# First chunks of x and w1 cut into three transfers, two of them on ScalarE's queue, and the products of two chunks ordered by terms

## The chip, the cores and the metric

The kernel runs on one core of a Trainium2 chip. The metric is device time in microseconds (us): the median of several executions. One execution was also profiled, and every row shown here is of that one.

## The reference

The block mixes two branches of the same x (2048 rows, D = 448) by a gate per row:

```
g = sigmoid(sum(x * gate_w))
a = linear_attention(x; wqkv, wo)        # 16 heads, phi(t) = where(t > 0, t + 1, exp(t)) + 1e-6
h = x @ w1 + b1;  r = max(h, 0);  b = (r * r) @ w2 + b2        # w1: 448 x 1792
out = g * a + (1 - g) * b
```

All data are float32. What the change touches is the very first product, h = x @ w1 for the first 512 rows of x.

## The kernel before

Every float32 operand is split into a high part (a copy into the type that TensorE multiplies at full pace, called `hi`, `xh`, `w[:, c]`) and a low part (the float32 value minus the high part: `lo`, `xl`, `w[:, 4 + c]`). A product is then three matmuls: high x high, high x low and low x high. ScalarE (ACT) or VectorE (DVE) makes the high part, VectorE the low one.

x comes in transposed blocks of 512 rows (`TB`), each cut along the contracted dimension into 4 chunks of 128 partitions (c = 0 to 3). w1 comes in halves and groups of columns; group 0 of half 0 has 512 columns, 4 tiles of 128 (f = 0 to 3), and 4 chunks as well. The start of the program computes the four tiles `h_ps` (f = 0 to 3, `first`) of block 0. It begins with 14 matmuls on constants (`warm_ps`, L177), which need no data. Then chunk 0: its halves of x and w1 lie beside each other in one tensor `xw` of two parts, loaded by SyncE's queue (SP) into `xw_raw[0]` and `xw_raw[1]`. Part 0 holds 256 of the 512 columns of x and 256 of the 512 columns of w1, part 1 the rest. From part 0 ScalarE makes `xh[:, :256]` and VectorE `w[:, 0, :256]`; then the tiles f = 0 and 1 are multiplied with 256 columns each (L547), again for part 1, and then all that is left of chunk 0 with 512 columns (L229 in `up_chunk`): the high products of f = 2 and 3, the four `xl` products and the four of w1's low part. Chunks 1 to 3 follow, f by f with all terms of an f together. After them come the key product (`k_ps`) and the second product of the same block (`o_ps`).

TensorE, ScalarE and VectorE execute in the order in which the program is written. The order on SP is settled by the scheduler of the framework, which is free to put a transfer that waits for nothing ahead of others. A transfer occupies the queue while it is issued. SP and ScalarE can each issue transfers. Raw inputs share 15 buffers (`slot`); `gw_s` (gate_w, copied to all 128 partitions) and `b1_s` have buffers of their own.

Of the kernel before, what the change touches and what calls it, by code (L numbers as in the profile page):

```python
# [7 lines left out]
F = mybir.dt.float32  # L8
R = mybir.dt.float32r
AF = mybir.ActivationFunctionType  # L10
# [5 lines left out]
P = 128  # L16
TB = 512
# [8 lines left out]
def f32(ap):  # L26
    return ap.bitcast(F)


@with_exitstack  # L30
def gated_mix_kernel(ctx: ExitStack, tc: tile.TileContext, xw, xt, xn, wk, wq, wv, wo, w1a, w1b, w2, b1, b2, gw,
                     hmask, kvmask, halves, out):
    nc = tc.nc
    act, dve, pool, pe, sp = nc.scalar, nc.vector, nc.gpsimd, nc.tensor, nc.sync
# [6 lines left out]
    rest = ctx.enter_context(tc.tile_pool(name="rest", bufs=1, side="right"))  # L41
# [6 lines left out]
    def bank(name):  # L48
        turn[0] ^= 1
        return ms_p.tile([P, 512], F, name=name, tag=f"ms{turn[0]}")  # L50
# [3 lines left out]
    def slot(shape, dt, name):  # L54
        return work.tile(shape, dt, name=name, tag="s", bufs=NSLOT)

    def load(dst, src):
        sp.dma_start(out=dst, in_=src)
# [4 lines left out]
    def split_hi(eng, hi, src):  # L63
        if eng is act:
            act.activation(hi, src, AF.Copy)  # L65
        elif eng is pool:
            pool.tensor_scalar(hi, src, 1.0, 0.0, op0=ALU.mult, op1=ALU.add)
        else:
            eng.tensor_copy(hi, src)  # L69

    def split_lo(eng, lo, src, hi):
        eng.tensor_tensor(lo, src, f32(hi), op=ALU.subtract)  # L72
# [29 lines left out]
    x_raw, xs = {}, {}  # L102

    def load_x(b, c):
        x_raw[b, c] = slot([P, TB], F, f"xr{b}_{c}")
        load(x_raw[b, c], xt[b, c])

    def new_x(b):
        return [keep.tile([P, 4, TB], R, name=f"x{p}{b}", tag=f"x{p}", bufs=2) for p in "hl"]

    def split_x(b, c):
        if c == 0:
            xs[b] = new_x(b)
        (xh, xl), r = xs[b], x_raw[b, c]
        if c < 3:
            split_hi(act, xh[:, c], r)
            split_lo(dve, xl[:, c], r, xh[:, c])
        else:
            split_last(xh[:, 3], xl[:, 3], r, side)
# [8 lines left out]

    w1_s, w1_raw = {}, {}

    def load_w1(h, g, c):
        w1_raw[h, g, c] = slot([P, (TB, 3 * P)[g]], F, f"w1r{h}{g}{c}")
        load(w1_raw[h, g, c], (w1a, w1b)[g][h, c])

    def new_w1(h, g):
        n, a, z = ((TB, 0, 16), (3 * P, 48, 0))[g]
        w = keep.tile([P, a + 7 * n + z], R, name=f"w1_{h}{g}", tag=f"w1{g}", bufs=1)
        w1_s[h, g] = w[:, a:a + 7 * n].rearrange("p (c n) -> p c n", c=7)
        return w1_s[h, g]

    def split_w1(h, g, c):
        if c == 0:
            new_w1(h, g)
        split_w(w1_s[h, g], c, w1_raw.pop((h, g, c)), act, dve)
# [7 lines left out]
    def split_w2(f):  # L152
        w2_s[f] = keep.tile([P, 2, D], R, name=f"w2_{f}", tag="w2", bufs=NH)
        split_hi(act, w2_s[f][:, 0], w2_raw[f])
        split_lo(dve, w2_s[f][:, 1], w2_raw.pop(f), w2_s[f][:, 0])
# [20 lines left out]
    for _ in range(14):  # L176
        pe.matmul(warm_ps[:, :256], warm[:, :P], warm, start=True, stop=True)  # L177

    side = rest.tile([P, 56], F, name="side")[:, :2]
    dve.memset(side[:64, 0:1], -1.0)  # L180
    dve.memset(side[:64, 1:2], 0.0)
    dve.memset(side[64:], 1.0)

    xw_raw = []
    for n in range(2):
        xw_raw.append(slot([P, TB], F, f"xwr{n}"))
        load(xw_raw[n], xw[n])
    for c in range(1, 4):
        load_x(0, c)
        load_w1(0, 0, c)  # L190
    b1_s = keep.tile([P, NF], F, name="b1_s")
    half = keep.tile([P, 2], F, name="half")
    ones = keep.tile([P, 2], F, name="ones")
# [8 lines left out]
    for c in range(4):  # L202
        load_w1(0, 1, c)
# [14 lines left out]
    def up_chunk(ps, b, f, c, only=None):  # L218
        h, fl = divmod(f, NH)
        g, i = divmod(fl, 4)  # L220
        w, cols = w1_s[h, g], slice(i * P, (i + 1) * P)
        xh, xl = xs[b]
        if c < 3:
            terms = [(w[:, c, cols], xh[:, c]), (w[:, c, cols], xl[:, c]), (w[:, 4 + c, cols], xh[:, c])]
        else:
            terms = [(w[:, 3, cols], xh[:, 3]), (w[:, 3, cols], xl[:, 3])]
        for n, (a, m) in enumerate(terms):
            if only in (None, n):
                pe.matmul(ps, a, m, start=(c == 0 and n == 0), stop=(c == 3 and n == 1))  # L229
# [155 lines left out]
    kv, wv_s, kvm = [], [], []  # L385

    def load_kv(c):
        if c == 0:
            kvm.append(slot([JE, D], F, "kvm"))
            load(kvm[0], kvmask)  # L390
        wv_s.append(slot([P, D], F, f"wv{c}"))
        load(wv_s[-1], wv[c])

    def kv_product():
        kv_ps = bank("kv_ps")
        z_ps = mm_p.tile([P, 512], F, name="z_ps", tag="mm")
        for c in range(4):
            pe.matmul(z_ps[:, 2 * c:2 * c + 2], zks[0][:, c].rearrange("p j r -> p (j r)"), ones, start=True,  # L398
                      stop=True)
        dve.tensor_copy(zc, z_ps[:, 0:8:2])  # L400
        for j in range(NJ):
            js = slice(j * JE, (j + 1) * JE)
            for c in range(4):
                pe.matmul(kv_ps[:JE, js], wv_s[c][:, js], gsum[c][:, js], start=(c == 0), stop=(c == 3))  # L404
        raw = slot([JE, D], F, "kv_raw")
        dve.tensor_tensor(raw, kv_ps[:JE, :D], kvm[0], op=ALU.mult)
        return raw.rearrange("p (j k) -> p j k", j=NJ)
# [126 lines left out]

    first = [mm_p.tile([P, 512], F, name=f"h_ps0_{f}", tag="mm") if f < 2 else bank(f"h_ps0_{f}") for f in range(4)]
    for c in range(4):
        if c == 0:
            xs[0] = new_x(0)  # L540
            w, (xh, xl) = new_w1(0, 0), [x[:, 0] for x in xs[0]]
            sides = slice(0, TB // 2), slice(TB // 2, TB)
            for n, cols in enumerate(sides):
                split_hi(act, xh[:, cols], xw_raw[n][:, sides[0]])
                split_hi(dve, w[:, 0, cols], xw_raw[n][:, sides[1]])
                for f in range(2):
                    pe.matmul(first[f][:, cols], w[:, 0, f * P:(f + 1) * P], xh[:, cols], start=(n == 0), stop=False)  # L547
            for m, (lo, hi) in enumerate(((xl, xh), (w[:, 4], w[:, 0]))):
                for n, cols in enumerate(sides):
                    split_lo(dve, lo[:, cols], xw_raw[n][:, sides[m]], hi[:, cols])  # L550
        else:
            split_x(0, c)
            split_w1(0, 0, c)
        if c == 0:
            for n in range(3):
                for f in range(0 if n else 2, 4):
                    up_chunk(first[f], 0, f, c, n)
        else:
            for f in range(4):
                up_chunk(first[f], 0, f, c)  # L560
    split_w2(0)
    split_w2(1)
    wk_s = keep.tile([P, 7, D], R, name="wk_s", tag="wkm", bufs=1)
# [53 lines left out]
    for b in range(1, NB):  # L617
        for f in range(NH):
# [36 lines left out]
            if b == 2:  # L655
# [4 lines left out]
                if f == 5:  # L660
                    raw = slot([P, P], F, "hmr")
# [3 lines left out]
            if b == 3:  # L665
                if f < 4:
                    load_w1(1, 0, f)
                if f == 4:
                    for c in range(4):
                        split_w1(1, 0, c)  # L670
                if f >= 2:
                    load_w2(NH + f - 2)
                if f >= 3:
                    split_w2(NH + f - 3)
                if f == 5:
                    key_sums()
                if f >= 5:
                    load_kv(2 * f - 10)
                    load_kv(2 * f - 9)
# [5 lines left out]
    for n, b in enumerate(order):  # L685
        then = order[n + 1] if n + 1 < NB else None
        for f in range(NF - NH, NF):
# [43 lines left out]
            if n == 0:  # L731
                if fl < 4:
                    todo += queries(b, (3, 0, 1, 2)[fl])
                if fl == 0:
                    for c in range(4):
                        load_w1(1, 1, c)
                    raw = kv_product()
# [91 lines left out]
```

## Time and profile before

| | |
|---|---|
| median of 3 executions | 435.35 us (435.15 to 435.68) |
| profiled execution, its own time | 435.59 us |
| span in the profile, first to last instruction | 433.8 us |
| TensorE (PE) matmul busy | 429.5 us, 99% |
| VectorE busy | 283.7 us, 65% |
| ScalarE busy | 174.5 us, 40% |
| GpSimd busy | 72.1 us, 17% |
| mean of the transfers | 67 GB/s |

The profiled execution took 1.8 us more than its span, and its time lies 0.24 us above the median. Matmuls are pipelined, so their recorded durations overlap: what one costs is the distance from its start to the next start, and a busy share of 99% says that there is hardly a gap, not that the clock is high.

### The profile page before, as it was taken

The numbers are of one execution on the slowest core, as the hardware profiler recorded it, in microseconds if no ns is written. First come the engines' busy times: TensorE is split into PE (matmuls) and PEld (weight loads), VectorE is DVE, ScalarE is ACT, GpSimd is POOL, SyncE is SP. The second block draws the span as 40 slices with busy tenths as digits, with TensorE's granted clock in tenths as the row PEclk, the third lists the DMA queues.
The fourth block names the chain that finished last, engine by engine and source line by source line (L and its number), as shares of the span: only waits on it lengthen the run. The fifth ranks groups of instructions, "written<-read, shape, count | busy, mean of one in ns | idle before, by whom it ended". The sixth has DMA issues, their size and how long they took to land.

```text
span 433.8 us, 5561 instructions
## 1 busy us (share of the span) xinstructions
PE 429.5 (99%) x2052; PEld 381.4 (88%) x2052; DVE 283.7 (65%) x462; ACT 174.5 (40%) x302; POOL 72.1 (17%) x93
## 2 busy tenths in 40 slices
PE   9999999999999999999999999999999999999996
PEld 7898999898989899898898888988888888888986
DVE  5899518843499437784449777887653967457624
ACT  6865324421346122453145443444433434233421
POOL 0045006500065002540010441000100001000000
PEclk9999999999999999999999999999999999999999
DMA  7741302020221211223244321130101301002002
GB/s 282 240 134 51 109 0 69 27 68 1 70 82 65 72 45 48 65 58 111 63 118 134 69 65 38 61 122 0 26 0 48 136 0 26 0 0 86 0 2 85
DMA packets 18347, 29.00 MB, mean 67 GB/s; under 512 B 2896, under 2 KB 12672, under 8 KB 18320
## 3 DMA queue, kind: packets, MB, share of 16 engines
q1 hardware_dynamic: 16416, 26.35, 19.5%
q0 software_dynamic: 1760, 2.20, 2.3%
q8 instruction: 16, 0.26, 0.3%
q14 instruction: 11, 0.09, 0.1%
q10 hardware_dynamic: 144, 0.10, 0.1%
HBM read 22.31 MB, written 3.67 MB: 60 GB/s over the span
## 4 chain that ended last, share of the span: by engine, by line
PE 98%; DMA 1%; DVE 0%; ACT 0%; DVEq 0%; issue 0%
PE h_ps L229 32%; PE o_ps L254 31%; PE q_ps L84 8%; PE k_ps L254 8%; PE a_ps L84 8%; PE g_ps L84 8%; PE kv_ps L404 1%; DMA xwr<-in_xw 1%; PE m_ps L84 1%; PE d_ps L84 0%; PE h_ps L547 0%; PE z_ps L398 0%; DVE out L278 0%; ACT xh L65 0%; DVEq L825 0%
## 5 line engine op out<-in xcount | busy, mean ns | idle before, releaser
L254 PE MATMUL o_ps<-w,hh 128*128 128x448 f32 x448 | 128.6, 362 | 0.0
L229 PE MATMUL h_ps<-xh,w 128*128 128x512 f32 x390 | 124.8, 391 | 0.0
L254 PEld LDWEIGHTS o_ps<-w,hh 128*128 128x128 f32 x448 | 84.0, 187 | 7.7
L229 PE MATMUL h_ps<-xl,w 128*128 128x512 f32 x224 | 87.0, 391 | 0.0
L229 PEld LDWEIGHTS h_ps<-xh,w 128*128 128x128 f32 x390 | 73.4, 188 | 14.1
L254 PE MATMUL o_ps<-w,hl 128*128 128x448 f32 x224 | 81.2, 362 | 0.0
L233 ACT ACTIVATE hr<-h_ps,b_s 128x512 f32<-128x512 f32 x56 | 38.1, 680 | 86.1 <-PE h_ps L229 80.8
L69 DVE CAST hh<-hr 128x512 fp32r<-128x512 f32 x56 | 23.5, 420 | 61.8 <-ACT hr L234 61.7
L229 PEld LDWEIGHTS h_ps<-xl,w 128*128 128x128 f32 x224 | 42.4, 189 | 8.0
L254 PEld LDWEIGHTS o_ps<-w,hl 128*128 128x128 f32 x224 | 42.0, 188 | 3.7
L72 DVE TENSOR_TENSOR hl<-hr,hh 128x512 fp32r<-128x512 f32 x56 | 39.7, 709 | 3.3
L72 POOL TENSOR_TENSOR nl<-xnr,nh 128x384 fp32r<-128x384 f32 x16 | 17.2, 1076 | 119.0 <-ACT nh L65 118.9
L234 ACT ACTIVATE hr<-hr 128x512 f32<-128x512 f32 x56 | 35.4, 632 | 1.8
L84 PE MATMUL q_ps<-xh,wq_s 128*128 128x512 f32 x100 | 33.1, 390 | 0.0
L84 PE MATMUL a_ps<-m_s,qh 128*128 128x448 f32 x112 | 32.7, 362 | 0.0
L254 PE MATMUL k_ps<-wk_s,xh 128*128 128x448 f32 x112 | 32.7, 361 | 0.0
L474 POOL DMA_DIRECT2D qr<-qv x16 | 7.9, 503 | 124.3 <-ACT qv L471 94.5
L72 DVE TENSOR_TENSOR pl<-r,ph 128x448 fp32r<-128x448 f32 x16 | 23.7, 1479 | 0.0
L327 POOL TENSOR_TENSOR ksum<-ksum,r 128x448 f32<-128x448 f32 x15 | 23.3, 1555 | 1.1 <-DVE r L289 1.1
L84 PE MATMUL q_ps<-xl,wq_s 128*128 128x512 f32 x60 | 23.4, 389 | 0.0
L254 PE MATMUL k_ps<-wk_s,xl 128*128 128x448 f32 x64 | 23.2, 363 | 0.0
L84 PE MATMUL a_ps<-m_s,ql 128*128 128x448 f32 x64 | 23.2, 362 | 0.0
(111 smaller groups left out, 565.8 us busy)
## 6 DMA issues: line engine op xcount, KB each, us to landing
xr<-in_xt SPq DMA_DIRECT2D x27, 256.0 KB, 2.7
xnr<-in_xn SPq DMA_DIRECT2D x16, 224.0 KB, 2.5
out<-out SPq DMA_DIRECT2D x15, 224.0 KB, 1.9
w2r<-in_w SPq DMA_DIRECT2D x14, 224.0 KB, 2.7
w1r<-in_w1a SPq DMA_DIRECT2D x7, 256.0 KB, 2.7
w1r<-in_w1b SPq DMA_DIRECT2D x8, 192.0 KB, 3.3
m_s<-m POOLq DMA_DIRECT2D x12, 112.0 KB, 2.5
wqr<-in_wq SPq DMA_DIRECT2D x4, 256.0 KB, 2.7
```

The lines of the kernel that those rows point to most:

```text
L69: eng.tensor_copy(hi, src)
L72: eng.tensor_tensor(lo, src, f32(hi), op=ALU.subtract)
L84: pe.matmul(out_ps, a, b, start=(i == 0), stop=(i == n - 1))
L229: pe.matmul(ps, a, m, start=(c == 0 and n == 0), stop=(c == 3 and n == 1))
L233: act.activation(r, ps, AF.Relu, bias=b1_s[:, f:f + 1])
L234: act.activation(r, r, AF.Square)
L254: pe.matmul(ps, a, m, start=start, stop=stop)
L327: pool.tensor_tensor(ksum, ksum, p, op=ALU.add)
L404: pe.matmul(kv_ps[:JE, js], wv_s[c][:, js], gsum[c][:, js], start=(c == 0), stop=(c == 3))
L474: pool.dma_start(out=r[p + 16:p + 32], in_=v[p:p + 16])
```

## The change

Chunk 0 now comes in three transfers. `xw0` has 256 columns of x and 128 columns of w1 (one tile), `xw1` the other 256 columns of x and the next 128 columns of w1, and `w1c` the last 256 columns of w1. `xw0` and `xw1` stay on SP's queue. `w1c`, and behind it chunk 1 of w1, are issued by ScalarE, behind a new ACTIVATE of two columns (`spare`), whose table load comes ahead of them. In chunk 0 the engines change roles: VectorE makes x's high parts, ScalarE w1's. The tiles f = 0 and 1 are multiplied in the order f0, f0, f1, f1. In chunk 1 VectorE makes x's high part, ScalarE makes w1's in two halves, and the products go by terms: first the high products of all four tiles, then the four with `xl`, then the four with w1's low part. The load of `kvm` moves from SP's queue to GpSimd's.

```diff
-    def load_w1(h, g, c):
+    def load_w1(h, g, c, queue=sp):
         w1_raw[h, g, c] = slot([P, (TB, 3 * P)[g]], F, f"w1r{h}{g}{c}")
-        load(w1_raw[h, g, c], (w1a, w1b)[g][h, c])
+        queue.dma_start(out=w1_raw[h, g, c], in_=(w1a, w1b)[g][h, c])
...
-    side = rest.tile([P, 56], F, name="side")[:, :2]
+    side, spare = [t[:, n:n + 2] for t in [rest.tile([P, 56], F, name="side")] for n in (0, 2)]
...
-    for n in range(2):
-        xw_raw.append(slot([P, TB], F, f"xwr{n}"))
-        load(xw_raw[n], xw[n])
+    for n, src in enumerate((xw0, xw1, w1c)):
+        xw_raw.append(slot([P, src.shape[1]], F, f"xwr{n}"))
+        if n < 2:
+            load(xw_raw[n], src)
+        else:
+
+            act.activation(spare, nc.const_aps.tensor(1.0, (P, 2), F), AF.Copy)
+            act.dma_start(out=xw_raw[n], in_=src)
+            load_w1(0, 0, 1, act)
     for c in range(1, 4):
         load_x(0, c)
-        load_w1(0, 0, c)
+        if c > 1:
+            load_w1(0, 0, c)
...
-            load(kvm[0], kvmask)
+            pool.dma_start(out=kvm[0], in_=kvmask)
...
-            sides = slice(0, TB // 2), slice(TB // 2, TB)
-            for n, cols in enumerate(sides):
-                split_hi(act, xh[:, cols], xw_raw[n][:, sides[0]])
-                split_hi(dve, w[:, 0, cols], xw_raw[n][:, sides[1]])
-                for f in range(2):
-                    pe.matmul(first[f][:, cols], w[:, 0, f * P:(f + 1) * P], xh[:, cols], start=(n == 0), stop=False)
-            for m, (lo, hi) in enumerate(((xl, xh), (w[:, 4], w[:, 0]))):
-                for n, cols in enumerate(sides):
-                    split_lo(dve, lo[:, cols], xw_raw[n][:, sides[m]], hi[:, cols])
+            hx = TB // 2
+            xcols, wcols = (slice(0, hx), slice(hx, TB)), (slice(0, P), slice(P, 2 * P), slice(2 * P, TB))
+            for n in range(2):
+                split_hi(dve, xh[:, xcols[n]], xw_raw[n][:, :hx])
+                split_hi(act, w[:, 0, wcols[n]], xw_raw[n][:, hx:])
+            split_hi(act, w[:, 0, wcols[2]], xw_raw[2])
+            for f, n in ((0, 0), (0, 1), (1, 0), (1, 1)):
+                pe.matmul(first[f][:, xcols[n]], w[:, 0, wcols[f]], xh[:, xcols[n]], start=(n == 0), stop=False)
+            for n in range(2):
+                split_lo(dve, xl[:, xcols[n]], xw_raw[n][:, :hx], xh[:, xcols[n]])
+            for n, raw in enumerate((xw_raw[0][:, hx:], xw_raw[1][:, hx:], xw_raw[2])):
+                split_lo(dve, w[:, 4, wcols[n]], raw, w[:, 0, wcols[n]])
+        elif c == 1:
+            (xh, xl), w, rx, rw = xs[0], w1_s[0, 0], x_raw[0, 1], w1_raw.pop((0, 0, 1))
+            split_hi(dve, xh[:, 1], rx)
+            for cols in (slice(0, 2 * P), slice(2 * P, TB)):
+                split_hi(act, w[:, 1, cols], rw[:, cols])
+            split_lo(dve, xl[:, 1], rx, xh[:, 1])
+            split_lo(dve, w[:, 5], rw, w[:, 1])
         else:
             split_x(0, c)
             split_w1(0, 0, c)
-        if c == 0:
-            for n in range(3):
-                for f in range(0 if n else 2, 4):
-                    up_chunk(first[f], 0, f, c, n)
-        else:
-            for f in range(4):
-                up_chunk(first[f], 0, f, c)
+        for n in range(3) if c < 2 else (None,):
+            for f in range(2 if (c, n) == (0, 0) else 0, 4):
+                up_chunk(first[f], 0, f, c, n)
```

On SP's queue, from its first transfer on, the order before was this (`xwr` are the parts of chunk 0, `xr` chunks of x, `w1r` chunks of w1, `b_s` here b1):

```order
L58 DMA xwr_110<-in_xw 128x512
L58 DMA xwr_112<-in_xw 128x512
L58 DMA xr_1_114<-in_xt 128x512
L58 DMA w1r_116<-in_w1a 128x512
L58 DMA xr_2_118<-in_xt 128x512
L58 DMA w1r_120<-in_w1a 128x512
L58 DMA xr_3_122<-in_xt 128x512
L58 DMA w1r_124<-in_w1a 128x512
L58 DMA b_s<-in_b 128x14
```

With the change the same place reads:

```order
L58 DMA xwr_110<-in_xw 128x384
L58 DMA xwr_112<-in_xw 128x384
L58 DMA b_s<-in_b 128x14
L58 DMA gw_s<-in_gw 128x448
L58 DMA xr_1_119<-in_xt 128x512
L58 DMA xr_2_121<-in_xt 128x512
L133 DMA w1r_123<-in_w1a 128x512
L58 DMA xr_3_125<-in_xt 128x512
L133 DMA w1r_127<-in_w1a 128x512
```

The scheduler has put b1 and the copied `gw_s` ahead of chunk 1 of x; before, `gw_s` was the 20th transfer of this queue. Chunk 1 of w1 has left it.

On ScalarE's queue the program began like this (`w_00` is the split w1 of half 0, group 0):

```order
L65 ACT_TABLE_LOAD
L65 ACTIVATE xh_169<-xwr_110 128x256
L65 ACTIVATE xh_169<-xwr_112 128x256
L65 ACTIVATE xh_169<-xr_1_114 128x512
L65 ACTIVATE w_00_171<-w1r_116 128x512
```

and it begins like this with the change:

```order
L191 ACT_TABLE_LOAD
L191 ACTIVATE side<-const-float32-1.0 128x2
L192 DMA xwr_114<-in_w1c 128x256
L133 DMA w1r_117<-in_w1a 128x512
L65 ACTIVATE w_00_174<-xwr_110 128x128
L65 ACTIVATE w_00_174<-xwr_112 128x128
L65 ACTIVATE w_00_174<-xwr_114 128x256
L65 ACTIVATE w_00_174<-w1r_117 128x256 x2
```

The two transfers stand between the table load with its two-column ACTIVATE and the first split. On TensorE, behind the 14 matmuls on constants, the program before had (`h_ps_0` to `h_ps_3` are the four tiles):

```order
L547 MATMUL h_ps_0_165<-xh_169,w_00_171 128x256
L547 MATMUL h_ps_1_166<-xh_169,w_00_171 128x256
L547 MATMUL h_ps_0_165<-xh_169,w_00_171 128x256
L547 MATMUL h_ps_1_166<-xh_169,w_00_171 128x256
L229 MATMUL h_ps_2_167<-xh_169,w_00_171 128x512
L229 MATMUL h_ps_3_168<-xh_169,w_00_171 128x512
L229 MATMUL h_ps_0_165<-xl_170,w_00_171 128x512
```

and the changed one has:

```order
L557 MATMUL h_ps_0_168<-xh_172,w_00_174 128x256 x2
L557 MATMUL h_ps_1_169<-xh_172,w_00_174 128x256 x2
L236 MATMUL h_ps_2_170<-xh_172,w_00_174 128x512
L236 MATMUL h_ps_3_171<-xh_172,w_00_174 128x512
L236 MATMUL h_ps_0_168<-xl_173,w_00_174 128x512
```

The number and the shapes of the products are the same; the second product now needs `xw1`, and the fifth needs `w1c`.

## Rows read from the trace of the kernel before

**Rows 1.** The page: span, and busy time of each engine.

```profile
span 433.8 us, 5561 instructions
PE 429.5 (99%) x2052; PEld 381.4 (88%) x2052; DVE 283.7 (65%) x462; ACT 174.5 (40%) x302; POOL 72.1 (17%) x93
```

**Rows 2.** The page: the chain that ended last, shares by engine.

```profile
PE 98%; DMA 1%; DVE 0%; ACT 0%; DVEq 0%; issue 0%
```

**Rows 3.** Waits of TensorE over the span, then TensorE's weight loads in 0 to 25.

```profile
PE warm_ps L177 <- PEq L821: 0.8, 1, 0.8
...
PEld h_ps L547 <- ACT xh L65: 0.5, 1, 0.5
```

**Rows 4.** Timeline of TensorE's matmuls from 0 to 9.5: start, duration, instruction.

```profile
0.78 3.15 PE L177 MATMUL warm_ps<-const-bfloat16-1.0 128*128 128x256 bf16 x14 [0.78 <-PEq L821]
...
3.51 0.42 PE L177 MATMUL warm_ps<-const-bfloat16-1.0 128*128 128x256 bf16 x1
3.98 1.39 PE L547 MATMUL h_ps<-xh,w 128*128 128x256 f32 x4
5.17 1.05 PE L229 MATMUL h_ps<-xh,w 128*128 128x512 f32 x2
6.02 1.38 PE L229 MATMUL h_ps<-xl,w 128*128 128x512 f32 x4
7.24 1.31 PE L229 MATMUL h_ps<-xh,w 128*128 128x512 f32 x5
8.38 0.39 PE L229 MATMUL h_ps<-xl,w 128*128 128x512 f32 x1
8.61 0.62 PE L229 MATMUL h_ps<-xh,w 128*128 128x512 f32 x2
9.06 0.39 PE L229 MATMUL h_ps<-xl,w 128*128 128x512 f32 x1
```

**Rows 5.** Timeline of ScalarE and VectorE, 0 to 8.

```profile
0.74 1.28 ACT L65 ACT_TABLE_LOAD   x1 [0.74 <-PEq L821]
...
3.51 0.42 ACT L65 ACTIVATE xh<-xwr 128x256 fp32r<-128x256 f32 x1 [1.49 <-DMA xwr<-in_xw]
3.51 0.29 DVE L69 CAST w<-xwr 128x256 fp32r<-128x256 f32 x1 [2.40 <-DMA xwr<-in_xw]
...
4.11 0.42 ACT L65 ACTIVATE xh<-xwr 128x256 fp32r<-128x256 f32 x1 [0.18 <-DMA xwr<-in_xw]
...
5.96 0.63 ACT L65 ACTIVATE xh<-xr 128x512 fp32r<-128x512 f32 x1 [1.44 <-DMA xr<-in_xt]
...
6.66 0.63 ACT L65 ACTIVATE w<-w1r 128x512 fp32r<-128x512 f32 x1
```

**Rows 6.** Timeline of SP's issues.

```profile
0.74 0.85 SPq L58 DMA_DIRECT2D xwr<-in_xw  x2
...
1.64 0.43 SPq L58 DMA_DIRECT2D xr<-in_xt  x1
2.11 0.43 SPq L58 DMA_DIRECT2D w1r<-in_w1a  x1
...
11.12 0.42 SPq L58 DMA_DIRECT2D gw_s<-in_gw  x1
```

**Rows 7.** Transfers of 0 to 25: count, KB each, median us from issue to landing.

```profile
xr<-in_xt SPq DMA_DIRECT2D x3, 256.0 KB, 4.7
...
xwr<-in_xw SPq DMA_DIRECT2D x2, 256.0 KB, 2.8
gw_s<-in_gw SPq DMA_DIRECT2D x1, 224.0 KB, 5.9
```

**Rows 8.** Stretches: last columns are granted clock, DMA share, GB/s.

```profile
2.00:3.00 1.00, 1.00 (x7) 0.72 (x5) 0.00 (x0) 0.02 (x1) 0.00 (x0) 1.00 0.89 311
...
12.00:13.00 1.00, 1.00 (x6) 0.83 (x5) 1.00 (x3) 1.00 (x3) 0.00 (x0) 1.00 1.08 401
...
14.50:15.00 0.50, 0.50 (x4) 0.42 (x3) 0.50 (x1) 0.47 (x2) 0.00 (x0) 1.00 1.08 165
15.00:15.50 0.50, 0.50 (x4) 0.42 (x3) 0.11 (x1) 0.50 (x1) 0.00 (x0) 1.00 0.84 115
15.50:16.00 0.50, 0.50 (x4) 0.47 (x3) 0.36 (x1) 0.50 (x2) 0.00 (x0) 1.00 1.21 89
16.00:16.50 0.50, 0.50 (x4) 0.46 (x4) 0.47 (x2) 0.47 (x2) 0.00 (x0) 1.00 0.74 176
```

**Rows 9.** Timeline of VectorE, then of TensorE, 12 to 19.

```profile
12.77 2.34 DVE L72 TENSOR_TENSOR wk_s<-wkr,wk_s 128x448 fp32r<-128x448 f32 x4
15.64 0.43 DVE L69 CAST hh<-hr 128x512 fp32r<-128x512 f32 x1 [0.53 <-ACT hr L234]
16.10 0.69 DVE L72 TENSOR_TENSOR hl<-hr,hh 128x512 fp32r<-128x512 f32 x1
...
17.22 0.36 PE L254 MATMUL k_ps<-wk_s,xh 128*128 128x448 f32 x1
17.62 0.56 PE L254 MATMUL o_ps<-w,hh 128*128 128x448 f32 x2
18.02 0.36 PE L254 MATMUL o_ps<-w,hl 128*128 128x448 f32 x1
```

**Rows 10.** Instructions on the tile kvm: duration min/median/max, first and last start.

```profile
L58 SPq DMA_DIRECT2D kvm<-in_kvmask x1: 342/342/342, 193.5 to 193.5; - x1
L406 DVE TENSOR_TENSOR kv_raw<-kv_ps,kvm x1: 625/625/625, 221.3 to 221.3; 112x448 f32<-112x448 f32 x1
```

More of the change, by code (lines that the diff above doesn't have):

```diff
@@ L30, in gated_mix_kernel @@
 @with_exitstack
-def gated_mix_kernel(ctx: ExitStack, tc: tile.TileContext, xw, xt, xn, wk, wq, wv, wo, w1a, w1b, w2, b1, b2, gw,
+def gated_mix_kernel(ctx: ExitStack, tc: tile.TileContext, xw0, xw1, w1c, xt, xn, wk, wq, wv, wo, w1a, w1b, w2, b1, b2, gw,
                      hmask, kvmask, halves, out):
@@ L801 @@
     a = {
-        "xw": np.stack([np.concatenate([t[:, n * TB // 2:(n + 1) * TB // 2] for t in (xt[0, 0], w1[0, 0])], axis=1)
-                        for n in range(2)]),
+        "xw0": np.concatenate([xt[0, 0, :, :TB // 2], w1[0, 0, :, :P]], axis=1),
+        "xw1": np.concatenate([xt[0, 0, :, TB // 2:], w1[0, 0, :, P:2 * P]], axis=1),
+        "w1c": w1[0, 0, :, 2 * P:TB],
         "xt": xt,
```

## The prediction

> **What bounds the kernel now.** I read the page first: TensorE is busy for 429.5 of 433.8 us [rows 1], and the chain that ended last is TensorE's for 98% of the span [rows 2]. Then its waits: over the whole span its matmuls waited once, 0.8 us for the start of the program; its weight loads add one wait of 0.5 us, for the first high part of x [rows 3]. After that nothing makes TensorE wait, so the time is its work and the pace of that work. A shorter transfer or a quicker split pays only if the first products start earlier.
>
> The pace has to be read from distances between starts. The 14 matmuls on constants start at 0.78 to 3.51 [rows 4]: 0.21 us for 256 columns, which is the 1.2 GHz level. Two products of 512 columns lie between 5.17 and 6.02, 0.425 us each: the same level. Between 8.38 and 9.06 there are three, 0.227 us each: the 2.4 GHz level. Four start between 6.02 and 7.24; 1.6 slow and 2.4 quick ones fill these 1.22 us, so the step to the upper level was at about 6.7. The granted clock stands at 1.00 in the stretch 2 to 3 as well [rows 8], where the starts show the lower level; I trust the starts. TensorE had been at work almost without a gap since 0.78 when the step came.
>
> From this follow two prices. Work shifted by 1 us ahead of the step is worth 0.227/0.425 = 0.53 us at the end. A step that comes 1 us later costs 0.47 us.
>
> **The change part by part.**
>
> *Start of the first product.* The second part of chunk 0 was split 0.60 us after the first (3.51 and 4.11) [rows 5], so 256 KB cost 0.60 us. A first transfer that is smaller by 64 KB should be usable at 3.36. VectorE's cast takes 0.29 us; ScalarE's copy of 128 columns some 0.31 us (256 took 0.42 and 512 took 0.63, so 0.21 per 256). Both are done by 3.7. The last constant matmul began at 3.51 and lasts 0.21 us, so the first product begins at about 3.74 in place of 3.98 [rows 4].
>
> *The next three.* `xw1` is smaller by as much again: usable at 3.81, cast at 4.10. The four products of 256 columns took 1.19 us, 0.30 each. The second can go at 4.12, so the fifth, the first that needs `w1c`, could go at 5.02; before it went at 5.17. The best case of these two edits is therefore 0.15 us ahead of the step: 0.08 us at the end.
>
> *The third transfer.* The trace has no transfer that stands behind a table load, so I bound its issue. It can't be earlier than 0.74, where the load begins. The latest that rows allow is 3.51, where the first ACTIVATE behind the load began, though that one waited for a transfer [rows 5]. I take the end of the load, 2.02, plus at most 0.2 us for the two-column ACTIVATE. From issue to landing, the first transfers took 2.8 us and the next ones, behind others, 4.7 [rows 7]; half the size saves some 0.3. I take 2.7, because the queue of ScalarE is empty, and landing at 4.85. With 0.42 us for the split, the fifth product goes at 5.3, later than before by 0.13 us: +0.07 us at the end. The ends of the range: landing before 4.55 gives the 5.02 above, -0.08 us; issue at 2.2 and 4.7 us to landing give 7.3, where 1.5 us of work ahead of the step (0.8 us at the end) and 0.6 us behind it are lost, +1.4 us.
>
> The edit's own saving is an issue of 0.43 us on SP [rows 6]; what counts is how the transfers share their engines, and 2 to 3 moved 311 GB/s with SP's queue alone, 12 to 13 moved 401 [rows 8]. On this the Trainium skill, "DMA: Bandwidth & Descriptors", section "Issuing engines are not separate DMA queues", speaks against the change: transfers of all queues run on the same 16 engines and interleave, and a second issuer saves only the time of issuing. By that rule the 384 KB on ScalarE's queue gain nothing over SP's and take their share from `xw1` or from chunk 1; no row here has two queues at once. By the rule the sum stays near zero too, unless they run beside `xw1`, which is the second rival.
>
> *Chunk 1.* x's part now waits behind b1 and `gw_s` on SP. Before, both parts of chunk 1 were there by 6.66 [rows 5]. The 224 KB of `gw_s` at 401 GB/s add 0.57 us: 7.25. VectorE's cast of 512 columns is at most twice that of 256, 0.58: ready at 7.8. The first product of chunk 1 went at 8.15 (7.24 and four steps of 0.227) and goes at 8.2: hidden, by 0.4 us. The other bound: `gw_s`, issued at 11.12 and landed 5.9 later [rows 6, 7], passed through a stretch in which 16 engines moved 136 GB/s on average, from 14.5 to 16.5 [rows 8]. Against 401 that is 1.32 us lost. Another copied row (b2) was on its way as well; half of it is 0.66 us, and x would be ready at 8.5, 0.3 us too late at full clock; all of it makes 0.95 us. I take the quick end, because there the 16 engines had two such loads at once.
>
> *Edits that cost nothing.* The order by terms in chunk 1 asks for `xl` and the low part of w1 four products, 0.9 us, later each, so it loosens waits that were met already. The extra ACTIVATEs (0.2 us of fixed cost each) fall into ScalarE's idle time, 1.44 us before 5.96 [rows 5]. Later splits move by 0.6 us, with SP's later transfers: the key weights' low parts were done at 15.1 and are used up to 17.22; `hh` was ready at 16.07 for 17.62, `hl` at 16.79 for 18.02 [rows 9]. Some 1.2 us cover that; beyond it every us would be lost whole. `kvm` was issued at 193.5 and read at 221.3 [rows 10]; a slower queue is hidden by 27 us.
>
> *Sum:* +0.07 us. The profiled execution (435.59) would become 435.66, and the median, which lies 0.24 lower, **435.4 us**. That can't be told from no change: about 0.2%, 0.9 us, is what a measurement of this kernel can tell. Its own range, from the quick ends to a wait of 0.5 us, is 434.9 to 436.0.
>
> **The rivals.**
>
> 1. *ScalarE's queue issues late* (slower). If the two transfers leave at 3.5, `w1c` lands at 6.2 and is split by 6.65: TensorE stands still from 5.0 to 6.7. All 1.5 us of work ahead of the step are lost, 0.8 us: 436.2. If the pause also delays the step, by as much as it lasts, 0.7 us more: 436.9. It decides from a split later than 6.75. For it: the first ACTIVATE is seen only at 3.51. Against: it waited for `xw`, and the load's row ends at 2.02. The Trainium skill, "ScalarE: Activation LUTs", section "What ACT_TABLE_LOAD costs", gives about 1.28 us for the load, as the row does, and a further 1.38 us of drain, which no run here shows; by it the ACTIVATE would start at 3.40. Chance 0.13.
>
> 2. *The queue runs past the load* and issues at 0.8. Then `w1c` and `w1r` share the engines with `xw1`: 128 to 256 KB ahead of it, 0.3 to 0.6 us. The second product goes at 4.4 to 4.7, the fifth at 5.3 to 5.6: +0.07 to +0.23 us, 435.5. For it: nothing in the program makes the issue wait. Chance 0.12.
>
> 3. *x's chunk 1 comes late behind `gw_s`*: +0.3 to +0.95 us, 435.9 as a middle. Chance 0.09.
>
> 4. *The step of the clock comes later* with small pauses alone, at the second and the fifth product. It decides from 1.85 us later (0.47 each): 436.3 to 437. The row of before shows a pause of 0.26 us and a step all the same. Chance 0.07.
>
> 5. *The step comes earlier*, because the pause between constants and products goes. From 1.85 us earlier, at 4.85, it is worth 0.87 us: 434.5. Nothing in the rows asks for it. Chance 0.06.
>
> **How the numbers follow.** The forecast has what is left, 0.53. Slower by over 0.2%: rival 4, most of rival 1 (0.10), a third of rival 3, and the forecast's tail (0.02): 0.22. Faster: rival 5 and a little of the forecast's lower tail, 0.07. The rest, 0.71, lies within 0.2%. The range runs from 434.8 (which leaves out rival 5 and a few hundredths of the forecast) to 436.9, the price of rival 1 with a late step; the rarer combinations above it are left out.
>
> **What would show it.** The first product starts at 3.7 to 3.8. ScalarE's first DMA issue stands behind the end of the table load, near 2.1 (0.8 would be rival 2, 3.4 rival 1). TensorE's fifth product starts at 5.0 to 5.6 and waits on ScalarE's split of `w1c`. No wait of TensorE behind 9 us; chunk 1 begins near 8.2, without a wait for x's cast (with one: rival 3). The spacing of the starts falls from 0.425 to 0.227 us near 6.7; elsewhere, rival 4 or 5. The prediction is wrong if the clock's step moves by 2 us or `w1c` is usable only after 6.75.

## The result and the profile after

The changed kernel is slower: 437.31 us, the median of 20 executions (436.85 to 439.38), against 435.47 us of the kernel before in the same comparison (20 executions, three of them above 436.4). The ratio is 1.0047, with a 95% interval of [1.0038, 1.0055]. That lies above the predicted range of 434.8 to 436.9. The profiled execution took 437.43 us, 1.84 more than that of before.

The page of the changed kernel, against [rows 1, 2]: the span, and the shares of the chain that ended last.

```profile
span 435.7 us, 5567 instructions
...
PE 97%; DMA 2%; SPq 0%; DVE 0%; issue 0%; DVEq 0%
```

The span grew by 1.9 us, and the share of DMA in the chain from 1% to 2%. The waits of TensorE (line, what it waited for, us in total, times, longest) say where:

```profile
PE warm_ps L177 <- PEq L836: 0.8, 1, 0.8
PE h_ps L236 <- DVE xh L69: 0.5, 1, 0.5
PE h_ps L557 <- DVE xh L69: 0.5, 1, 0.5
```

Before, the first of these was the only one [rows 3]. Both new waits are for a high part of x. The timeline of TensorE's matmuls gives their places:

```profile
3.82 0.55 PE L557 MATMUL h_ps<-xh,w 128*128 128x256 f32 x1
4.84 1.01 PE L557 MATMUL h_ps<-xh,w 128*128 128x256 f32 x3 [0.47 <-DVE xh L69]
5.64 1.05 PE L236 MATMUL h_ps<-xh,w 128*128 128x512 f32 x2
6.50 1.91 PE L236 MATMUL h_ps<-xl,w 128*128 128x512 f32 x4
8.20 1.20 PE L236 MATMUL h_ps<-xh,w 128*128 128x512 f32 x4
9.91 1.16 PE L236 MATMUL h_ps<-xh,w 128*128 128x512 f32 x4 [0.51 <-DVE xh L69]
10.91 0.39 PE L236 MATMUL h_ps<-xl,w 128*128 128x512 f32 x1
```

The first product starts at 3.82 (3.98 before), but the second waits until 4.84. The four products from 6.50 to 8.20 cost 0.425 us each, the lower level of the clock; before, the step to the upper level came at about 6.7 [rows 4]. Here it comes at about 8.4, among the last four of chunk 0 (from 8.20). Chunk 1 then begins at 9.91 behind a second wait, where before it began at 8.15 (by the working of the prediction). These 1.76 us, and 0.09 us for the next four (1.00 us to 10.91 in place of four times 0.227), make 1.85 us: the whole difference. Behind 11 us the products keep that distance to those of before, so nothing more was lost.

The timelines of ScalarE (with its queue, ACTq) and VectorE show what TensorE waited for:

```profile
0.74 1.28 ACT L191 ACT_TABLE_LOAD   x1 [0.74 <-PEq L836]
0.80 0.38 ACTq L192 DMA_DIRECT2D xwr<-in_w1c  x1
1.20 0.45 ACTq L133 DMA_DIRECT2D w1r<-in_w1a  x1
2.03 0.20 ACT L191 ACTIVATE side<-const-float32-1.0 128x2 f32<-128x2 f32 x1
...
3.38 0.29 DVE L69 CAST xh<-xwr 128x256 fp32r<-128x256 f32 x1 [2.26 <-DMA xwr<-in_xw]
4.49 0.29 DVE L69 CAST xh<-xwr 128x256 fp32r<-128x256 f32 x1 [0.82 <-DMA xwr<-in_xw]
...
9.34 0.43 DVE L69 CAST xh<-xr 128x512 fp32r<-128x512 f32 x1 [3.15 <-DMA xr<-in_xt]
```

ScalarE's queue issued `w1c` at 0.80, beside the table load. `xw0` was usable at 3.38, `xw1` only 1.11 us later. Chunk 1 of x was cast at 9.34; before it was split at 5.96 [rows 5]. The chain in order of time (start, us, what) and the stretches (last columns: DMA share and GB/s) say why:

```profile
2.59 6.72 DMA xr<-in_xt
...
9.91 4.13 PE h_ps L236 x17
```

```profile
3.00:4.00 1.00, 1.00 (x6) 0.52 (x4) 0.29 (x1) 0.31 (x1) 0.00 (x0) 1.00 1.04 384
4.00:5.00 1.00, 0.53 (x2) 0.24 (x2) 0.51 (x2) 0.51 (x2) 0.00 (x0) 1.00 1.18 173
5.00:6.00 1.00, 1.00 (x4) 0.97 (x5) 1.00 (x5) 0.72 (x3) 0.00 (x0) 1.00 0.42 89
```

Chunk 1 of x was 6.72 us on its way (4.3 before: issued at 1.64 [rows 6], split at 5.96 [rows 5]); meanwhile the 16 engines fell from 384 to 173 and 89 GB/s, much like the 89 to 176 that [rows 8] had shown where `gw_s` and b2 passed. Two things had thus gone wrong: a pause at the second product with a late clock step, and x late behind `gw_s`. They overlap: without the wait for x, chunk 1 would have begun near 9.2 (8.20, one product across the step, three of 0.227 us), 1.06 us late by the first alone; the wait adds 0.7 us.

The 20 executions lie in two groups, 16 from 436.85 to 437.69 and four from 438.85 to 439.38. In three of those four the mean granted clock is 0.996, in all others 0.999 or 1.000. The run that has both causes and fills the pause (e10_gw_fill, below) shows what that probably is.

### The profile page after: what moved, and what is told of

The parts are those of the page before. It is cut to its first block, busy times and chain, and to the rows that moved or that the text cites. A ratio compares the mean times of both kernels' runs of the same rounds, so it can differ in the third digit from the quotient of the medians.

```text
span 435.7 us, 5567 instructions
## 1 busy us (share of the span) xinstructions
PE 430.5 (99%) x2052; PEld 381.8 (88%) x2052; DVE 283.7 (65%) x464; ACT 174.1 (40%) x304; POOL 72.6 (17%) x94
## 4 chain that ended last, share of the span: by engine, by line
PE 97%; DMA 2%; SPq 0%; DVE 0%; issue 0%; DVEq 0%
PE h_ps L236 32%; PE o_ps L261 31%; PE q_ps L84 8%; PE g_ps L84 8%; PE a_ps L84 8%; PE k_ps L261 8%; DMA xr<-in_xt 2%; PE kv_ps L411 1%; PE m_ps L84 1%; PE d_ps L84 0%; SPq L58 0%; PE z_ps L405 0%; DVE out L285 0%; DVE xh L69 0%; DVEq L840 0%
```

## The experiments

My theory was that each of the two causes alone costs over 1 us. The rivals: that one of them does nothing, that 224 KB of any kind would hold up x as much, or that the step goes by time and not by TensorE's pauses. Ratios are against the kernel before on the same chip. Shares of executions are given because the times of several of these kernels lie in two groups, below 436.4 and above 436.8.

### e1_gw_held: the copied rows held back

The memsets keep both copied rows behind the key weights' splits; b1 and a tiny transfer take the free places on SP's queue.

```diff
+    for t in (gw_s, b2_s):
+        dve.memset(t[:, :1], 0.0)
     load(gw_s, gw.partition_broadcast(P))
     load(b2_s, b2.partition_broadcast(P))
```

> The changed kernel with the two copied rows (gw_s, b2) held behind the split of the key weights. Theory 1 (the copied gate row ahead of x's chunk 1 sets the loss): x's chunk 1 lands by 7.2 us instead of 9.3, TensorE no longer waits at the start of chunk 1, which begins near 9.2 instead of 9.9; 0.7 us less, about 436.6. Rival (the pause at the second product and the late clock step are the whole loss): the wait for x goes, but nothing is gained, 437.2 to 437.4. Both expect xw1 usable near 4.5 still, since ScalarE's transfers still run beside it.

Measured: 437.11 us, ratio 1.0027 [1.0012, 1.0042]; three of 12 executions at 435.13 to 435.56, the other nine at 436.83 to 438.20. Its timelines of VectorE and of TensorE:

```profile
7.08 0.43 DVE L69 CAST xh<-xr 128x512 fp32r<-128x512 f32 x1 [0.52 <-DMA xr<-in_xt]
```

```profile
5.21 1.01 PE L557 MATMUL h_ps<-xh,w 128*128 128x256 f32 x3 [0.46 <-DVE xh L69]
6.02 1.05 PE L236 MATMUL h_ps<-xh,w 128*128 128x512 f32 x2
6.88 1.91 PE L236 MATMUL h_ps<-xl,w 128*128 128x512 f32 x4
8.58 2.06 PE L236 MATMUL h_ps<-xh,w 128*128 128x512 f32 x8
```

x's chunk 1 comes 2.3 us earlier (7.08 for 9.34) and chunk 1 begins without a wait: that is the price of the copied row in these two executions. The pause at the second product is still there, and the lower level still lasts until 8.58 at least. So the median moved by only 0.2 us, less than I expected, though a quarter of the executions fell to the time of before. In most, the pause costs the whole loss without the row. The two prices of the prediction account for most of it in the profiled one: a step some 2 us later (8.7 for 6.7) makes 0.94 us, a fifth product 0.85 us later (6.02 for 5.17) 0.45 us, and chunk 1 begins 1.4 us later (near 9.55 for 8.15). The last 0.3 us of its difference arose behind 200 us.

### e2_all_sp: all three transfers on SP

```diff
-            act.activation(spare, nc.const_aps.tensor(1.0, (P, 2), F), AF.Copy)
-            act.dma_start(out=xw_raw[n], in_=src)
-            load_w1(0, 0, 1, act)
+            load(xw_raw[n], src)
+            load_w1(0, 0, 1)
```

w1's chunk 1 goes back to SP as well, and the spare ACTIVATE, which only served ScalarE's queue, is left out.

> Three transfers, roles and order of products as changed, but the third transfer and chunk 1 of w1 go back to SP's queue, in that order behind xw1; the two-column ACTIVATE goes. With nothing taken off SP the scheduler leaves the copied rows at the 21st place. Theory (both parts of the loss come from the second queue: sharing with xw1, and the gap on SP that the copied row fills): xw1 usable at 3.8, the fifth product at 5.0, chunk 1 without a wait near 8.0, 435.3 or a little less than before. Rival (roles, small transfers or the order by terms cost by themselves): above 436.

Measured: 437.36 us, ratio 1.0033 [1.0021, 1.0046], four of 12 executions below 436.0. My expectation failed. The splits of chunk 0 on ScalarE, then TensorE:

```profile
3.14 0.31 ACT L65 ACTIVATE w<-xwr 128x128 fp32r<-128x128 f32 x1 [1.12 <-DMA xwr<-in_xw]
3.62 0.31 ACT L65 ACTIVATE w<-xwr 128x128 fp32r<-128x128 f32 x1 [0.17 <-DMA xwr<-in_xw]
5.50 0.42 ACT L65 ACTIVATE w<-xwr 128x256 fp32r<-128x256 f32 x1 [1.57 <-DMA xwr<-in_w1c]
```

```profile
5.97 1.22 PE L235 MATMUL h_ps<-xh,w 128*128 128x512 f32 x2 [0.99 <-ACT w L65]
6.99 1.91 PE L235 MATMUL h_ps<-xl,w 128*128 128x512 f32 x4
8.70 2.65 PE L235 MATMUL h_ps<-xh,w 128*128 128x512 f32 x8
```

`xw1` now follows `xw0` by 0.48 us in place of 1.11, so ScalarE's 384 KB had indeed taken their share from it (and from `xw0`, usable at 3.14 in place of 3.38). But `w1c`, third on SP, is usable only 3.9 us after its issue at 1.64, and the pause moves to the fifth product and doubles. The products from 6.99 to 8.70 are at the lower level again. Here no copied row is ahead of x; the pause alone suffices. The rival's time came true, above 436, but not for its reason: e4_fill and e7_third_only keep the roles, the small transfers and the order by terms, and lie at 435.4 and 435.6.

### e4_fill: the pause filled

The kernel of e1_gw_held, with three matmuls on constants in the pause (a wait of 0.34 us is left of it in the rows below).

```diff
             for f, n in ((0, 0), (0, 1), (1, 0), (1, 1)):
+                for _ in range(3 if (f, n) == (0, 1) else 0):
+                    pe.matmul(warm_ps[:, :256], warm[:, :P], warm, start=True, stop=True)
                 pe.matmul(first[f][:, xcols[n]], ...
```

> The changed kernel with the copied rows held, and three constant matmuls between TensorE's first and second product, where it paused for 0.5 us and more. If the pause is what puts the clock's step off from 6.6 to 8.4 us: the step returns to about 6.7, and 0.8 us is gained over the same kernel without the three, about 435.8. If the step's time has other reasons: no gain, 436.6, as without them.

Measured: 435.39 us, ratio 1.0003 [0.9994, 1.0012]; ten of 11 executions at 435.05 to 435.75, one at 437.31. TensorE:

```profile
4.37 0.51 PE L558 MATMUL warm_ps<-const-bfloat16-1.0 128*128 128x256 bf16 x3
5.21 0.62 PE L559 MATMUL h_ps<-xh,w 128*128 128x256 f32 x3 [0.34 <-DVE xh L69]
5.67 0.63 PE L236 MATMUL h_ps<-xh,w 128*128 128x512 f32 x2
6.13 1.09 PE L236 MATMUL h_ps<-xl,w 128*128 128x512 f32 x4
```

The median fell by 1.7 us against e1_gw_held, through matmuls whose results nobody reads: ten of 11 executions now take the time of before, where it was three of 12, and the three matmuls are the only edit between the two kernels. That is what shows the price of the pause. The profiled execution shows what an early step is worth. The second product starts as late as in e1_gw_held (5.21); yet from 5.67 on, products of 512 columns cost 0.23 us, so chunk 1 begins near 8.0 in place of 9.55. The late product cost little; what cost was the clock. But it doesn't show that the filling brings the step, for its three constants take 0.51 us together, where at the lower level they would take 0.84 (two steps of 0.21 and one duration of 0.42 [rows 4]). The upper level was there at 4.4 already, as the pause began. This is also why more came back than the 0.8 us that I had expected from a step at 6.7.

### e8_before_10_const: a pause in the kernel before

```diff
-    for _ in range(14):
+    for _ in range(10):
         pe.matmul(warm_ps[:, :256], warm[:, :P], warm, start=True, stop=True)
```

> The kernel before with 10 in place of 14 matmuls on constants: TensorE stands still from 2.9 to 3.9, no transfer and no split is changed. Theory (a pause near 1 us ahead of the products puts the clock step off): most executions at 436.6 to 437.3, profile with a step at 8 or later, ratio 1.003 to 1.004. Rival (the step goes by the transfers or by time, not by pauses): 435.4, ratio within 0.0005 of 1.

Measured: 436.46 us (435.98 to 437.69), ratio 1.0029 [1.0019, 1.0038].

```profile
3.98 1.40 PE L547 MATMUL h_ps<-xh,w 128*128 128x256 f32 x4 [0.91 <-ACT xh L65]
5.18 1.06 PE L229 MATMUL h_ps<-xh,w 128*128 128x512 f32 x2
6.03 1.69 PE L229 MATMUL h_ps<-xl,w 128*128 128x512 f32 x4
7.56 1.32 PE L229 MATMUL h_ps<-xh,w 128*128 128x512 f32 x5
```

The products stand where they stood before (3.98, 5.18, 6.03), and no transfer changed. Only four matmuls without use are gone from ahead of them, and the kernel loses 1.1 us; none of its nine executions is under 435.98, where the kernel before has its median at 435.38. This settles the rival that the step goes by time or by the transfers alone. The profile is of the fastest of the nine: the four from 6.03 cost 0.38 us each (1.53 us to 7.56), which puts the step at about 7.4, 0.7 us later than in [rows 4] and not at 8 as I had expected; the slower ones have no trace. The median is a little below what I had expected. Here and in e4_fill the matmuls on constants change two things at once, the pause and the work ahead of the step; which of the two counts was not separated.

### e9_before_15_const: the small pause of before filled

One more matmul on constants, 15 for 14.

> The kernel before with 15 in place of 14 matmuls on constants, which fills the pause of 0.26 us ahead of the first product. Theory (a shorter pause makes the early step surer): 435.0 to 435.4, and none of the executions above 436.2 that the kernel before has now and then. Rival (0.26 us make no difference): 435.4 with the same few.

Measured: 435.16 us, ratio 1.0 [0.9991, 1.0009]; one of 11 executions still at 437.20. The median came out as expected but can't be told from no change, and the surer step was not seen: a pause of 0.26 us is not worth filling.

### e5_before_gw_early: the copied row in the kernel before

In the kernel before, `gw_s` becomes the third transfer of SP's queue; nothing else changes.

```diff
+    gw_s = keep.tile([P, D], F, name="gw_s")
+    load(gw_s, gw.partition_broadcast(P))
     for c in range(1, 4):
         load_x(0, c)
         load_w1(0, 0, c)
```

> The kernel before with one edit: the copied gate row is issued third on SP, ahead of chunk 1. Theory 1 (this row alone holds chunk 1): chunk 1 of x lands at 8 us or later instead of 5.9, TensorE waits for it at 8.2, and the kernel is 1 to 1.5 us slower, 436.4 to 437. Rival (it needs the second queue's transfers beside it): hidden by the 1.5 us that x's chunk 1 has to spare, no change, 435.4.

Measured: 436.70 us, ratio 1.0034 [1.0022, 1.0046], none of six executions under 436.34. ScalarE, then TensorE:

```profile
7.27 0.63 ACT L65 ACTIVATE xh<-xr 128x512 fp32r<-128x512 f32 x1 [2.79 <-DMA xr<-in_xt]
```

```profile
4.87 0.64 PE L230 MATMUL h_ps<-xh,w 128*128 128x512 f32 x2
...
8.59 0.50 PE L230 MATMUL h_ps<-xh,w 128*128 128x512 f32 x1 [1.26 <-ACT w L65]
```

TensorE waits for the split of w1, which ScalarE makes right behind that of x. In this execution the clock was up from 4.87 on at the latest, 1.8 us earlier than in [rows 4], and the time was nevertheless 0.9 us above the profiled one of before. Work that is done sooner only waits longer for chunk 1: the copied row alone sets a floor.

### e6_gw_plain: the same bytes without copying

```diff
-    load(gw_s, gw.partition_broadcast(P))
+    load(gw_s, wk[0])
```

> The changed kernel, but the place of gate_w on the queue is filled by 224 KB of plain rows (a block of the key weights, one row to each partition) in place of one row copied to 128 partitions; the gate is then computed with wrong weights. Theory (it is the copying of one row that holds up the engines): the engines keep 300 to 400 GB/s, x's chunk 1 is usable near 7.2, no wait at the start of chunk 1, and what is left is the late clock step: times at 435.1 to 435.6 or at 436.8 to 437.5, median 437.0. Rival (224 KB ahead of x are too much of whatever kind): x usable at 9 or later, a wait of 0.5 us or more, no execution under 436.8, median 437.3 as the changed kernel.

Measured: 435.96 us, ratio 1.0021 [1.0009, 1.0033]; seven of 12 executions at 435.21 to 436.01, five at 436.86 to 437.67. Stretches, VectorE and TensorE:

```profile
4.00:5.00 1.00, 0.33 (x1) 0.13 (x1) 0.17 (x1) 0.18 (x1) 0.00 (x0) 1.00 1.06 314
5.00:6.00 1.00, 0.83 (x5) 0.79 (x6) 1.00 (x5) 1.00 (x4) 0.00 (x0) 1.00 1.08 398
```

```profile
6.45 0.42 DVE L69 CAST xh<-xr 128x512 fp32r<-128x512 f32 x1
```

```profile
0.78 2.95 PE L177 MATMUL warm_ps<-const-bfloat16-1.0 128*128 128x256 bf16 x14 [0.78 <-PEq L836]
...
5.17 0.62 PE L557 MATMUL h_ps<-xh,w 128*128 128x256 f32 x3 [0.84 <-DVE xh L69]
```

With the same 224 KB in the same place the engines keep 314 and 398 GB/s (173 and 89 with the copied row), the transfer lands 3.6 us after its issue (6.6), and x is there when VectorE comes to it at 6.45. Chunk 1 begins without a wait. It is the copying of one row to 128 partitions that costs, not the bytes. The two groups of e1_gw_held remain, at the times that I had expected; the median lies under the expected 437.0 because seven executions fell into the lower one. The profiled execution is of that group (435.34): its 14 constants take 2.95 us in place of 3.15 [rows 4], so the upper level was there before the products, and the wait of 0.84 us at the second product, longer than the changed kernel's 0.47, cost nothing.

### e10_gw_fill: both causes at once, one of them undone

The changed kernel with the three matmuls of e4_fill and its `gw_s` left ahead of x.

> The changed kernel, queues untouched, with three matmuls on constants between the first and the second product, which fill the pause there. Theory (the late clock step and the copied row overlap; each alone costs nearly the whole): x's chunk 1 still begins at 9.7 to 10 behind a wait of 0.5 us or more, now at the upper level, and the time keeps the changed kernel's lower level, 436.8 to 437.5, without executions near 439; median 437.1. Rival (they add up, and filling the pause gives back what the step cost, 0.8 us): 436.3 to 436.6.

Measured: 438.06 us, ratio 1.0055 [1.0038, 1.0071]: three executions at 437.14 to 437.25 and three at 438.86 to 439.10. The floor held, so an earlier step gives nothing back while x is late, and the rival of 436.3 to 436.6 is out. But I had expected no execution near 439, and half of them are there, the profiled one among them. Its timeline of TensorE, and its stretches (granted clock third from the end):

```profile
6.93 1.08 PE L236 MATMUL h_ps<-xh,w 128*128 128x512 f32 x4
9.81 1.16 PE L236 MATMUL h_ps<-xh,w 128*128 128x512 f32 x4 [1.80 <-DVE xh L69]
10.82 1.73 PE L236 MATMUL h_ps<-xl,w 128*128 128x512 f32 x4
```

```profile
10.00:11.00 1.00, 1.00 (x5) 0.83 (x5) 1.00 (x3) 1.00 (x2) 0.00 (x0) 1.00 0.97 324
11.00:12.00 1.00, 1.00 (x4) 0.74 (x4) 1.00 (x2) 0.94 (x3) 0.00 (x0) 0.50 0.90 317
...
13.00:14.00 1.00, 1.00 (x3) 0.77 (x3) 0.97 (x2) 1.00 (x2) 0.00 (x0) 0.50 0.99 317
14.00:15.00 1.00, 1.00 (x5) 0.79 (x4) 0.97 (x3) 0.96 (x3) 0.00 (x0) 0.79 1.04 389
```

With the clock up early, chunk 0 is done by 8.0, TensorE stands still for 1.80 us, and the clock falls back to 0.50 from 11 on; the mean of 0.79 in the stretch 14 to 15 leaves 0.42 us of it at the lower level. The fall comes 1.2 us after the products went on at 9.81. These 3.4 us at half pace cost 0.47 each, 1.6 us, close to the distance of the two groups (1.7 us). The mean granted clock of this execution and of the two others near 439 is 0.996, as in three of the four slowest of the changed kernel. By this sign its upper group is mostly this fall, not a step that comes still later; no execution of that group was profiled there, so this is not shown. The fourth, with a mean of 1.000, must be something else, and what it is stays open.

### e7_third_only: only `w1c` on ScalarE's queue

e1_gw_held, with chunk 1 of w1 back on SP.

```diff
-            load_w1(0, 0, 1, act)
+            load_w1(0, 0, 1)
```

> The changed kernel with both copied rows held back behind the key weights' splits, and ScalarE issues only w1c; w1's chunk 1 is back on SP. Theory (384 KB on ScalarE's queue beside xw1 make the pause at the second product): with 128 KB beside it xw1 is usable at 4.0 to 4.2, the pause is 0.3 us or less, the clock step comes at 4.4 to 6.7 in most executions, no wait at chunk 1; median 435.3, most executions under 435.8. Rival (one transfer of the second queue is enough): xw1 at 4.5 or later, a pause of 0.4 us or more, median 436.8 to 437.2 with the two levels of the run with held rows.

Measured: 435.59 us, ratio 1.0008 [0.9999, 1.0016], all 11 executions at 435.20 to 436.35.

```profile
3.45 0.29 DVE L69 CAST xh<-xwr 128x256 fp32r<-128x256 f32 x1 [2.34 <-DMA xwr<-in_xw]
4.22 0.29 DVE L69 CAST xh<-xwr 128x256 fp32r<-128x256 f32 x1 [0.48 <-DMA xwr<-in_xw]
```

`xw1` follows `xw0` by 0.77 us: 0.48 with nothing on ScalarE's queue, 0.77 with 128 KB, 1.09 to 1.30 with 384 (five profiled runs, the changed kernel's 1.11 among them). TensorE shows no wait but that for the start of the program, and the group above 436.8 is gone. The loss of the change is undone with its main idea left in; nothing is won either.

### e11_third_fill: an attempt to beat both

e7_third_only with 15 matmuls on constants ahead of the products and two between the first and the second.

> A version that is meant to beat both: the changed kernel with only w1c on ScalarE's queue, w1's chunk 1 back on SP, both copied rows held, 15 matmuls on constants ahead of the products and two between the first and the second. Theory (what is left of the change is a start earlier by 0.1 us, with the step kept early): 435.0 to 435.4, ratio 0.9990 to 1.0, all executions under 436.3. Rival (the filling matmuls only push the products back): 435.6 or more, as with only w1c on ScalarE's queue.

Measured: 435.63 us, ratio 1.0006 [0.9997, 1.0014], all 11 executions at 435.14 to 436.44. It is no better than e7_third_only, as the rival said. No version here beats the kernel before by what a measurement can tell.

## Why the prediction was wrong

**Chunk 1 behind `gw_s`: this step failed, and it set the time.** The prediction took 0.57 us for 224 KB at 401 GB/s and called the result hidden by 0.4 us. The copied row cost x 2.2 to 2.9 us (9.34 in the changed kernel and 9.24 in e10_gw_fill; with the row held back 7.08 in e1_gw_held and 6.48 at the latest in e4_fill), more than the upper bound of 1.32 us. Chunk 1 went at 9.91, not at 8.2. The rows that it had for this bound were the right ones: [rows 8] showed 89 to 176 GB/s over 2 us. It shared that loss between two copied rows and took the quick end, though one row alone brings the engines to 173 and 89 GB/s. This was rival 3, at 0.09, priced at 0.3 to 0.95 us; in the kernel before the row alone costs 1.2 us (e5_before_gw_early against before), and in the changed kernel, with the late step under it, 1.85 us are lost.

**The clock's step: taken as fixed at 6.7, and this failed too.** It came at 8.4. Rival 4 had the mechanism at 0.07, with small pauses as its condition. The times of e4_fill and e8_before_10_const show it in both directions, with no transfer changed between the kernels compared: e1_gw_held against e4_fill, 1.7 us; e8_before_10_const against before, 1.1 us. In the changed kernel itself the late step is covered by the wait for x, and the two prices don't add up (e10_gw_fill). The prediction read from [rows 4] that a pause of 0.26 us did no harm; that is true, and e9_before_15_const says the same. What a longer pause does it asked only in rival 1, for 1.7 us and with a step put off by as much as the pause lasts; here a wait of 0.47 us goes with a step that is 1.7 us later.

**The third transfer: its issue was wrong, its time on the way right.** The issue came at 0.80, not 2.1: rival 2, at 0.12. With the 2.7 us to landing that the prediction had taken, `w1c` was there at 3.5 and not at 4.85, so it was no longer what the fifth product waited for; that went at 5.64, where the rival had 5.3 to 5.6. What the early issue cost was `xw1`: usable at 4.49 against a forecast of 3.81. For rival 2 the prediction priced a shift of the work, +0.07 to +0.23 us (measured: 0.47 us at the fifth product, by 0.53 makes 0.25), but left the clock out of it. There the rivals should have been chained: 2 makes the pause, and the pause makes 4. The rule of the Trainium skill, "DMA: Bandwidth & Descriptors", section "Issuing engines are not separate DMA queues", that transfers of all issuers interleave on the same 16 engines, agrees with the distances of `xw1` from `xw0`: 0.48 us with nothing on ScalarE's queue, 0.77 with 128 KB and 1.09 to 1.30 with 384 KB.

**What was right, and what was luck.** The edits taken at nothing were right: the order by terms, the extra ACTIVATEs, the later key weights and `kvm` brought no wait, for TensorE shows none behind 9.91. The price of 0.47 us for each us that a step comes later also fits the fall in e10_gw_fill. The start of the first product (3.82 for a forecast of 3.74, `xw0` usable at 3.38 for 3.36) was luck of this execution: in the four other profiled runs with the same first transfers `xw0` is usable at 3.51 to 3.77 and the first product starts at 3.95 to 4.21, hardly earlier than before (3.98). The smaller `xw0` gains only where nothing runs on ScalarE's queue (e2_all_sp: 3.14, first product at 3.58); the forecast had left out what the early issue takes from it.

**Open.** Three of 12 executions of e1_gw_held and four of 12 of e2_all_sp take the time of before despite the pause. The one profiled execution of that sort (e6_gw_plain) had its step before the pause; why the step comes at such different times in executions of one kernel was not settled. Nor is the copied row's price known closely. In e5_before_gw_early it is 1.3 us against the profile of before (7.27 for 5.96), but 2.3 and 2.5 us against e9_before_15_const and e8_before_10_const, which have the same transfers and split x at 5.00 and 4.79; so these runs show no difference from the 2.2 to 2.9 us of the changed kernel.

## What to carry to other kernels

When transfers leave a queue, look at what the scheduler puts into their places, and price a row copied to all partitions by the rate that it leaves to the others (89 to 173 GB/s in the changed kernel, 117 and 153 in e5_before_gw_early), not by its bytes. Ahead of the step of the clock, a pause of TensorE is not priced by its length but by what it does to the step: half a us cost 1.7 us in most executions, and three matmuls without use gave it back. The two losses at the start of this program didn't add up, since the later arrival hid the other; so undo such losses together before judging any one.

## What the runs showed of the hardware

- ScalarE's queue issues transfers while its table is being loaded: `w1c` at 0.80 and `w1r` at 1.20, in a load from 0.74 to 2.02. The two-column ACTIVATE started at 2.03, 0.01 us behind the load. The Trainium skill, "ScalarE: Activation LUTs", section "What ACT_TABLE_LOAD costs", has a drain of 1.38 us besides the load; at this place no run shows one.
- The granted clock not only rises late; in e10_gw_fill it fell back after TensorE, already at the upper level, had stood still for 1.80 us (0.50 from 11 to 14, and the upper level again in the stretch 14 to 15). A pause of 1.26 us in e5_before_gw_early's profiled execution brought no such fall.
- 14 matmuls on constants are worth more than the time that they bridge: with ten (e8_before_10_const), the products start at the same moment and the kernel takes 1.1 us more.
- In the profiled executions the step to the upper level comes anywhere from the end of the constants, near 3.5 (e6_gw_plain), to 8.4 (the changed kernel) and later (e2_all_sp). A wait of 0.84 us behind the step cost nothing in e6_gw_plain; a pause ahead of it went with a step at 8.4 or later in the changed kernel, e1_gw_held and e2_all_sp.
